# The load stage of a gated Hedgehog attention kernel: query and key weights first, blocks of w_phi from the host, x stores behind the x loads

## The chip, the cores and the metric

One core of a Trainium2 chip. The metric is the device time of one execution in microseconds (us), the median of several runs. TensorE is called PE, its weight loads PEld, VectorE DVE, ScalarE ACT, GpSimd POOL, and the engine that issues most transfers SP. Each engine runs its own list of instructions strictly in the order in which it was written out when the program was built; semaphores hold an instruction until what it needs is there.

## What is computed

With x of 2048 rows and 576 columns, all in float32:

```
xn  = layernorm(x)
q, k, v = heads of xn @ wqkv                      # 32 heads of 18
pq, pk  = q @ w_phi[h], k @ w_phi[h]              # w_phi: 32 x 18 x 18
phi_q, phi_k = [softmax(p), softmax(-p)] each
s   = ((phi_q (phi_k^T v)) / (phi_q (phi_k^T 1) + 1e-6)) @ wo
B   = (silu(xn @ w_gate) * (xn @ w_up)) @ w_down  # 4608 hidden columns
out = x + s * silu(B)
```

pq and pk are linear in xn, so the kernel folds w_phi into the query and key weights before it multiplies them with x ("fold").

## The kernel before, in words

Products that must be as exact as float32 are made of float32r parts: each operand is split into a high part (a cast on ACT) and a low part (a subtraction on DVE or POOL), and the products high-high, high-low and low-high are summed in PSUM. `split_rows` does this for a weight that lies in two full chunks of 128 rows and a tail of 32; the tail's correction is a third, narrow DVE instruction.

The 2048 rows of x are four blocks of 512 rows: blocks 0 and 1 form the first half (i = 0), blocks 2 and 3 the second (i = 1). A normalised and transposed block lies in two "places" of `xpool`, X10 and X11 for block 2, X12 and X13 for block 3, X00 to X03 for blocks 0 and 1; a place holds 128 partitions of 5 x 512 numbers (two high chunks, the tail, two low chunks).

The load stage, which is all that the change touches, does the following.

- `load_x(b)` loads a block as four tiles `xn` of 128 rows. `norm_stats` makes mean and variance on DVE (two BN_STATS and a BN_AGGR per tile), the square root on ACT and five small DVE steps behind it; for blocks 0 and 1 together one such chain serves eight tiles. `norm_block` scales the tiles (two on DVE, two on ACT), repeats the tail columns on POOL, transposes the block on PE (24 transposes into three PSUM tiles `tp`), and splits the result into the X places (ACT cast, DVE subtraction; the tails by DVE for block 3 and by POOL for the others). ACT stores an unsplit copy of the tails, `x_dram`.
- `load_fold(m)` loads key (m = 0) or query (m = 1) weights in five groups of 126 rows (the last has 72), `fold` multiplies each group on PE with the block-diagonal matrix PHI of seven heads (six matmuls a group into a `tp` tile, which the profile counts as twelve) and splits it into KVWH/KVWL or QH/QL. Before, POOL makes PHI from w_phi (`phi_s`) and a mask of ones.
- `early_weights` and `early_tile` use blocks 2 and 3 at once: for the first two chunks of 128 hidden columns they multiply gate and up with x (PSUM tiles `pe`, 14 matmuls of 512 columns for gate and 14 for up; a "half tile" here is both for one block). They depend on one x block and on two loads `raw`.
- `keep_clock(n)` issues n matmuls of zeros whose result nobody reads.
- `keep_x` stores three X places of the second half to `a_dram`; they are read back some 800 us later.

At the end of the stage PE starts the key products (`k_tile`, tile `p2`; "p L94" in the profile), which need the folded key weights and block 2, and from which on the change leaves the order on every engine as it is.

The order on the engines is set by a scheduler when the program is built: it works through the program with its own estimates of durations; `tc.high_priority()` lets an instruction go ahead, `tc.issue_after(x)` holds one behind x, and what is written is otherwise its preference. The chip does not reorder the lists. PSUM tiles `tp` exist three times, `xn` eight times, `wst` (weights as loaded) five times before; a new use waits until the readers of the old one are done. At most eight transfers of SP and ACT together are under way: each takes the next of eight semaphores (DMAHW0 to DMAHW7) and waits until that one's last transfer has landed.

## Time and profile before

| what | value |
|---|---|
| median of 3 runs | 1603.73 us (1602.67 to 1605.22) |
| profiled execution, its own time / span | 1603.6 us / 1601.7 us |
| PE busy in the span | 1590.1 us (99%) |
| DVE, ACT, POOL busy | 73%, 45%, 41% |
| idle matmuls (L148) | 31 from 1.00 us, 6 from 14.78 us |
| first transpose of block 2 / of block 3 | 11.40 / 29.56 us |
| fold of the key weights from / of the query weights from | 16.21 / 53.78 us |
| first key product on PE | 66.59 us |

The profile is one execution. A timeline row has its start, how long the merged pieces took, engine, line, operation, written tile <- read tiles, shapes, count, and in brackets the idle time before it with what ended it. A row of groups has count, busy time and mean duration in ns. A row of a stretch has its length and each engine's busy time with the instruction count. Matmul durations overlap, so a count of starts over a time tells the pace. An idle engine costs nothing unless the others wait for it.

### The profile page before, as it was taken

Reading aid. Unit: us, or ns where it says so; the run is one execution under the profiler, and the core shown is the slowest. Engines: PE = TensorE matmul, PEld = TensorE weight load, DVE = VectorE, ACT = ScalarE, POOL = GpSimd, SP = SyncE. Lnnn points to the kernel's source line nnn. Section 1 sums busy time; section 2 is a strip of 40 time slices with the busy share of each in tenths; the row PEclk is TensorE's granted clock in tenths of the full one; section 3 lists DMA queues with packets and bytes.
Section 4 is the critical chain, followed back from the end, with each engine's and each line's share of the span. In section 5 each row is a group of like instructions: output and inputs, shape, how many; then the busy total and the mean of one; then the engine's idle time right before and its main releaser. Section 6 shows DMA issues by size and latency. Waiting matters only on the chain.

```text
span 1601.7 us, 25319 instructions
## 1 busy us (share of the span) xinstructions
PE 1590.1 (99%) x9415; PEld 1420.7 (89%) x9415; DVE 1176.5 (73%) x1729; ACT 724.9 (45%) x1404; POOL 663.7 (41%) x714
## 2 busy tenths in 40 slices
PE   9999999999999999999999999999999999999998
PEld 6899998999988888888888888888888888888887
DVE  7777769889866778987777778635667656666577
ACT  5633345444435654544444444455343333333334
POOL 3676662434115535544535445223324324133133
PEclk9999999999999999999999999999999999999999
DMA  9522243436438454455545453874545565556435
GB/s 313 189 81 80 91 145 115 126 108 189 127 132 280 164 192 165 164 180 189 179 163 201 171 180 124 325 229 139 163 138 146 183 193 158 171 181 187 143 117 178
DMA packets 123181, 268.29 MB, mean 168 GB/s; under 512 B 12978, under 2 KB 54066, under 8 KB 121778
## 3 DMA queue, kind: packets, MB, share of 16 engines
q1 hardware_dynamic: 107612, 244.73, 46.5%
q0 software_dynamic: 3552, 12.59, 2.7%
q10 hardware_dynamic: 11894, 9.35, 1.8%
q8 instruction: 74, 1.21, 0.3%
q14 instruction: 49, 0.40, 0.1%
HBM read 167.53 MB, written 99.09 MB: 166 GB/s over the span
## 4 chain that ended last, share of the span: by engine, by line
PE 92%; DVE 3%; POOL 2%; DMA 2%; ACT 1%; issue 1%; SPq 0%; ACTq 0%; DVEq 0%; POOLq 0%
PE pd L875 25%; PE px L758 24%; PE pw L758 12%; PE py L758 6%; PE p L94 6%; PE pe L94 5%; PE p L651 4%; PE kvp L330 2%; PE po L631 2%; PE vx L418 1%; PE pt L625 1%; POOL slo L363 1%; PE vy L94 1%; PE vx L94 1%; DMA wst<-in_A_w_qk 0%
## 5 line engine op out<-in xcount | busy, mean ns | idle before, releaser
L875 PEld LDWEIGHTS pd<-dw,hh 128*128 128x128 f32 x3012 | 424.0, 188 | 22.2 <-ACT pd L922 1.5
L875 PE MATMUL pd<-dw,hh 128*128 128x288 f32 x3012 | 438.5, 295 | 1.4 <-ACT pd L922 0.7
L758 PE MATMUL px<-X,w 128*128 128x512 f32 x1512 | 386.5, 390 | 0.0
L758 PEld LDWEIGHTS px<-X,w 128*128 128x128 f32 x1512 | 274.6, 188 | 49.1 <-ACT s L787 2.3
L758 PE MATMUL pw<-X,w 128*128 128x512 f32 x744 | 190.7, 392 | 0.0
L758 PEld LDWEIGHTS pw<-X,w 128*128 128x128 f32 x744 | 138.6, 188 | 29.4
L792 DVE TENSOR_TENSOR s<-pw,s 128x512 f32<-128x512 f32 x126 | 86.4, 687 | 97.7 <-ACT s L787 86.4
L1029 DVE TENSOR_TENSOR acc<-pd,acc 128x576 f32<-128x576 f32 x128 | 96.2, 753 | 76.9 <-PE pd L875 76.4
L787 ACT COPY s<-px 128x512 f32<-128x512 f32 x126 | 73.6, 584 | 156.7 <-PE px L758 156.7
L61 DVE TENSOR_TENSOR hh<-ha,hh 128x512 fp32r<-128x512 f32 x140 | 111.3, 821 | 21.8 <-ACT hh L60 21.4
L60 ACT CAST hh<-ha 128x512 fp32r<-128x512 f32 x140 | 82.7, 619 | 87.6 <-PE pd L875 74.3
L1001 POOL TENSOR_TENSOR hb<-hb 128x512 f32<-128x512 f32 x34 | 46.5, 1367 | 160.6 <-DVE hb L804 159.6
L94 PE MATMUL pe<-X,wh 128*128 128x512 f32 x340 | 107.0, 395 | 0.3 <-ACT wh L64 0.3
L61 DVE TENSOR_TENSOR w<-ld,w 128x512 fp32r<-128x512 f32 (+1 forms) x96 | 80.5, 839 | 34.2 <-ACT w L60 32.9
L758 PE MATMUL px<-X,wt 128*128 128x512 f32 x252 | 98.1, 389 | 0.0
L758 PE MATMUL py<-X,w 128*128 128x512 f32 x378 | 97.0, 391 | 0.0
L988 POOL TENSOR_TENSOR h<-ha,hb 128x512 f32<-128x512 f32 x34 | 44.6, 1313 | 124.2 <-DVE ha L808 94.1
L1014 POOL TENSOR_TENSOR ha<-ha 128x512 f32<-128x512 f32 x34 | 52.6, 1563 | 97.2 <-DVE hh L61 97.2
L60 ACT CAST w<-ld 128x512 fp32r<-128x512 f32 (+1 forms) x96 | 52.8, 550 | 87.3 <-POOL ld L746 57.2
L812 ACT COPY py<-px 128x512 f32<-128x512 f32 x63 | 36.0, 572 | 103.8 <-PE px L758 74.9
L743 POOL TENSOR_TENSOR ts<-ld 128x256 f32<-128x256 f32 x32 | 27.6, 864 | 127.0 <-issue 71.4
L758 PEld LDWEIGHTS py<-X,w 128*128 128x128 f32 x378 | 67.8, 188 | 10.7
(286 smaller groups left out, 3256.1 us busy)
## 6 DMA issues: line engine op xcount, KB each, us to landing
w_dram<-w SPq DMA_DIRECT2D x90, 512.0 KB
w<-w_dram SPq DMA_DIRECT2D x90, 512.0 KB
wt<-t_dram SPq DMA_DIRECT2D x62, 336.0 KB
ld<-in_B_w_gu SPq DMA_DIRECT2D x32, 512.0 KB
rt<-in_B_w_down SPq DMA_DIRECT2D x33, 288.0 KB
rb<-in_B_w_down SPq DMA_DIRECT2D x33, 288.0 KB
w_dram<-w SPq DMA_DIRECT2D x30, 256.0 KB
w<-w_dram SPq DMA_DIRECT2D x30, 256.0 KB
```

The source lines that it names most:

```text
L60: nc.scalar.copy(hi, src)
L61: nc.vector.tensor_sub(lo, src, hi)
L94: last = nc.tensor.matmul(ps, l, r, start=n == 0, stop=n == len(pairs) - 1)
L651: nc.tensor.matmul(ps[:, 0:HALF], a[0:w, g, jc], bw[0:w, g, n], start=k == 0, stop=k == 3 * NG - 1)
L758: nc.tensor.matmul(ps, l, r, start=first and n == 0, stop=last and n == len(mm) - 1, skip_group_check=True)
L787: snaps.append(nc.scalar.copy(t, ps))
L792: nc.vector.tensor_add(t, ps, t)
L875: nc.tensor.matmul(ps, l, r, start=first and n == 0 and m == 0, stop=n == len(hs) - 1 and m == 2, skip_group_check=True)
L988: sub(s, g["h"][0][0], g["h"][0][1])
L1001: nc.gpsimd.tensor_add(a21, a21, g["h"][1][1])
L1014: sub(a12, a12, g["h"][0][0])
L1029: nc.vector.tensor_add(a2, pd[:, :, 0:HALF], a2)
```

## The change

The host lays w_phi out as five blocks of 126 x 126 with the heads on the diagonal, so that PHI is one load and POOL's products are gone. The key weights are the first loads on SP, then block 2, the query weights, the first gate and up weights, block 3. Weights come into the X0 places, three groups to a place, which are free until blocks 0 and 1 are transposed. The key fold stands before everything else; two groups of the query fold stand before block 2's transposes, three behind them. Of the idle matmuls 8 are left. The value weights have six buffers instead of five. The three `a_dram` stores are held behind the last x load. Line numbers of the load stage move by up to four; L216 (transposes) becomes L212, L249 (folds) L248, L186 (statistics) L182.

```diff
-    XB = [[xpool.tile([P, 5, BT], F32R, name=f"X{i}{j}") for j in range(4)] for i in range(2)]
+    XB = [None, [xpool.tile([P, 5, BT], F32R, name=f"X1{j}") for j in range(4)]]
...
-                phi_s = prep.tile([GW, NG, DH], F32, name="phi_s")
-                PHI = prep.tile([GW, NG, GH, DH], F32, name="PHI")
-                wf = w_phi.rearrange("h d f -> (h d) f")
+                PHI = prep.tile([GW, NG, GW], F32, name="PHI")
...
-                        nc.sync.dma_start(xn[:, 0:D], xf[i * P:(i + 1) * P, :])
+                        loads.append(nc.sync.dma_start(xn[:, 0:D], xf[i * P:(i + 1) * P, :]))
...
                     for g, (o, w) in enumerate(GROUPS):
-                        ws.append(prep.tile([GW, 6 * P], F32, name="wst", bufs=5))
-                        nc.sync.dma_start(ws[g][0:w], w_qk[m, o:o + w])
+                        if g % 3 == 0:
+                            rows = xpool.tile([P, 5, BT], F32, name=f"X0{2 * m + g // 3}").rearrange("p c n -> p (c n)")
+                        ws.append(rows[0:w, g % 3 * 6 * P:(g % 3 + 1) * 6 * P])
+                        nc.sync.dma_start(ws[g], w_qk[m, o:o + w])
...
-                keep_clock(31)
+                keep_clock(8)
+                nc.scalar.dma_start(PHI, w_phi)
+                nc.scalar.dma_start(ident, ident_in)
+                wk = load_fold(0)
                 xns = load_x(2)
-                nc.scalar.dma_start(phi_s[:, 0:4, :], wf[0:4 * GW, :].rearrange("(g p) f -> p g f", p=GW))
-                nc.scalar.dma_start(phi_s[0:D - 4 * GW, 4, :], wf[4 * GW:D, :])
-                for g, (o, w) in enumerate(GROUPS):
-                    nc.gpsimd.tensor_mul(PHI[0:w, g], phi_s[0:w, g, :].unsqueeze(1).to_broadcast([w, GH, DH]), mask[0:w])
-                wk = load_fold(0)
+                wq = load_fold(1)
+                nc.scalar.dma_start(mask, mask_in)
+                fold(wk, KVWH, KVWL, range(NG))
+                norm_stats([2], xns[0:4])
+                fold(wq, QH, QL, range(2))
+                _, rest, copy = norm_block(2, xns[0:4])
+                folded = fold(wq, QH, QL, range(2, NG))
+                first_weights = [early_weights(0, rest, copy)]
                 xns += load_x(3)
-                norm_stats([2], xns[0:4])
-                last, rest, _ = norm_block(2, xns[0:4])
-                with tc.issue_after(last.ins):
-                    keep_clock(6)
                 with tc.issue_after(rest.ins):
                     norm_stats([3], xns[4:8])
-                first_weights = [early_weights(0)]
-                fold(wk, KVWH[:, :, :, 0:D], KVWL[:, :, :, 0:D])
                 _, _, copy = norm_block(3, xns[4:8])
...
-                wq = load_fold(1)
-                fold(wq, QH, QL)
                 norm_block(1, xns[4:8])
-                for f in range(2):
-                    early_tile(f, 1, first_weights[f], store=nc.gpsimd, hold=None if f else norms[3])
+                with tc.issue_after(folded.ins):
+                    for f in range(2):
+                        early_tile(f, 1, first_weights[f], store=nc.gpsimd, hold=None if f else norms[3])
...
             def keep_x():
-                for n, j in enumerate((0, 1, 3)):
-                    nc.sync.dma_start(a_dram[n], XB[1][j].bitcast(F32))
+                with tc.issue_after(loads[-1].ins):
+                    for n, j in enumerate((0, 1, 3)):
+                        nc.sync.dma_start(a_dram[n], XB[1][j].bitcast(F32))
...
+    phi = np.zeros((NG, GH, DH, GH, DH), np.float32)
+    for h in range(H):
+        phi[h // GH, h % GH, :, h % GH] = np.asarray(inputs["A_w_phi"])[h]
...
+            "A_w_phi": phi.reshape(NG, GW, GW).transpose(1, 0, 2),
```

How this moves instructions, at three places. First PE, at the start of its list, behind the first idle matmuls. Before (`tp<-ident,xn` are transposes, `tp<-PHI,wst` a fold, `pe<-X_64` half tiles; X_64 is X10):

```order
L148 MATMUL pe<-idle 128x512
L216 MATMUL tp<-ident,xn 128x128 x24
L148 LDWEIGHTS idle
...
L249 MATMUL tp<-PHI,wst 128x126 x18
L94 MATMUL pe<-X_64,wh 128x512 x2
```

Now (X_118 and X_122 are key weights in X00 and X01, X_133 and X_137 query weights in X02 and X03, X_60 is X10):

```order
L147 MATMUL pe<-idle 128x512
L248 MATMUL tp<-PHI,X_118 128x126 x18
L248 MATMUL tp<-PHI,X_122 128x126 x6
L248 MATMUL tp<-PHI,X_122 128x72 x6
L248 MATMUL tp<-PHI,X_133 128x126 x12
L212 MATMUL tp<-ident,xn 128x128 x24
L248 MATMUL tp<-PHI,X_133 128x126 x6
L248 MATMUL tp<-PHI,X_137 128x126 x6
L248 MATMUL tp<-PHI,X_137 128x72 x6
L94 MATMUL pe<-X_60,wh 128x512
```

The transposes of block 2, which came first, stand behind the whole key fold and two groups of the query fold.

Second, DVE at the normalisation of block 2, from the last tile's statistics to the scaling. Before:

```order
L186 BN_STATS stats<-xn 128x6
L187 BN_AGGR mv<-stats 128x2 [waits DVE_49]
L190 TENSOR_SCALAR mv<-mv 128x4 [waits DVE_49]
L192 RECIPROCAL rs<-rs 128x4 [waits Activation_49]
L193 TENSOR_TENSOR rt<-rs 128x4 [waits DVE_49]
```

Now (QL and QH are the split of the first two query groups):

```order
L182 BN_STATS stats<-xn 128x6
L65 TENSOR_TENSOR QL<-tp,QH 128x4x126 [waits Activation_49]
L183 BN_AGGR mv<-stats 128x2 [waits DVE_49]
L66 TENSOR_TENSOR QH<-tp,QH 32x2x126
L186 TENSOR_SCALAR mv<-mv 128x4 [waits DVE_49]
L65 TENSOR_TENSOR QL<-tp,QH 128x4x126 [waits Activation_49]
L188 RECIPROCAL rs<-rs 128x4 [waits Activation_49]
L66 TENSOR_TENSOR QH<-tp,QH 32x2x126
L189 TENSOR_TENSOR rt<-rs 128x4 [waits DVE_49]
```

The two query groups now stand inside the chain that ends in the scale of block 2. On ACT, both QH casts and a table load stand before the square root in the same way.

Third, DVE at the normalisation of block 3, now. Between the steps of its root stand the statistics of block 0's first tiles, each with a wait for its load:

```order
L182 BN_STATS stats<-xn 128x6 [waits DMAHW1_49]
L186 TENSOR_SCALAR mv<-mv 128x4 [waits DVE_49]
L182 BN_STATS stats<-xn 128x6
L188 RECIPROCAL rs<-rs 128x4 [waits Activation_49]
L183 BN_AGGR mv<-stats 128x2 [waits DVE_49]
L182 BN_STATS stats<-xn 128x6 [waits DMAHW2_49]
L189 TENSOR_TENSOR rt<-rs 128x4 [waits DVE_49]
...
L182 BN_STATS stats<-xn 128x6 [waits DMAHW3_49]
...
L200 TENSOR_SCALAR xn<-xn,mv,rs 128x576 x2
```

Before, the root of block 3 was mixed with the splits of the key weights (KVWL, KVWH) instead, and the statistics of block 0 came behind the scaling.

18 lines of the change are left out of this document (9 added, 9 removed).

## The prediction

> **What bounds the kernel now.** I read the page first, then two stretches of the span (busy time of PE, PEld, DVE, ACT, POOL; granted clock, DMA share, GB/s), then the chain of waits, PE's timeline, and last DMA, DVE and ACT in the first part alone.
>
> ```profile
> 0.00:66.60 66.60, 62.82 (x366) 48.47 (x366) 51.78 (x118) 43.20 (x60) 25.30 (x53) 1.00 0.88 290
> 66.60:330.00 263.40, 262.94 (x1904) 250.67 (x1905) 207.60 (x290) 111.88 (x234) 151.25 (x182) 1.00 0.33 104
> ```
>
> From 66.6 us on PE idles 0.5 us in 263 us, and from there on the change leaves every engine its instructions in the same order. A shift of the first key product therefore moves the end by as much; nothing behind it takes a delay back. Only the first 66.6 us decide. The chain of waits, then PE's timeline, then the half tiles between 37 and 46 us:
>
> ```profile
> 5.28 7.74 DMA wst<-in_A_w_qk
> 66.59 3.99 PE p L94 x28
> ...
> 1.00 9.70 PE L148 MATMUL pe<-idle 128*128 128x512 bf16 x31 [1.00 <-POOL idle L143]
> 11.40 0.44 PE L216 MATMUL tp<-ident,xn 128*128 128x128 f32 x2 [0.70 <-DVE xn L204]
> 14.78 1.46 PE L148 MATMUL pe<-idle 128*128 128x512 bf16 x6
> 16.21 4.28 PE L249 MATMUL tp<-PHI,wst 126*128 126x126 f32 x36
> 29.56 2.81 PE L216 MATMUL tp<-ident,xn 128*128 128x128 f32 x24
> 53.78 5.52 PE L249 MATMUL tp<-PHI,wst 126*128 126x126 f32 x48
> 37.00:46.00 9.00, 9.00 (x41) 7.45 (x40) 0.69 (x1) 1.19 (x2) 1.00 1.02 372
> ```
>
> Useful PE work starts at 11.40 with the transposes of the first x block (block 2). It is four blocks of transposes (2.8 us each, 11.2 us), two folds of five groups (5.52/4 = 1.4 us a group, 7.0 us a fold) and four half tiles of gate and up (28 matmuls each; 9.00/41 = 0.22, by the starts 0.2275 us, so 6.4 us each, 25.5 us). That makes 50.7 us of the 55.2 us from 11.40 to 66.59. To be had are the first 11.4 us, the 1.5 us of idle matmuls and 3 us of gaps. DVE is nearly as full: it is busy 51.8 of 66.6 us, and between 15 and 50 us almost without a break. These are its groups in that window (count, busy us, mean ns):
>
> ```profile
> L186 DVE BATCH_NORM_STATS2 stats<-xn 128x6 f32<-128x288 f32 x24 | 9.3, 428 | 0.0
> L204 DVE TENSOR_SCALAR xn<-xn,mv,rs 128x576 f32<-128x576 f32 x5 | 2.9, 594 | 0.0
> L65 DVE TENSOR_TENSOR KVWL<-tp,KVWH 128x504 fp32r<-128x504 f32 x4 | 2.7, 670 | 0.1
> L187 DVE BATCH_NORM_AGGREGATE mv<-stats 128x2 f32<-128x12 f32 x12 | 2.4, 198 | 0.1
> L66 DVE TENSOR_TENSOR KVWH<-tp,KVWH 32x252 fp32r<-32x252 f32 x4 | 1.7, 418 | 0.1
> L228 DVE TENSOR_TENSOR X<-tp,X 32x512 fp32r<-32x512 f32 x2 | 1.3, 678 | 0.0
> ```
>
> **The change, part by part.** *Removed:* 29 of 37 idle matmuls, and POOL's five products for PHI (2 us, off the chain). That by itself gains nothing; it only lets the folds start when their operands land. *The x stores* (three of 1280 KB, 3.93 MB, 10.6 us at the 372 GB/s of the last PE row) go behind the x loads. I cost that at nothing, since DVE waited for x loads 4.7 us in all, 3.9 of them before the first tile:
>
> ```profile
> DVE stats L186 <- DMA xn<-in_A_x: 4.7, 3, 3.9
> ```
>
> Without that cover, it is the upper bound of a gain, 0.8 us; behind the loads the stores run while PE works, and their reader is in the second half.
>
> *When the work can start.* PE's order is now: fold K (five groups), two groups of fold Q, and only then the transposes of block 2. These can no longer come before the second query load has landed. DMA rates by stretch, and the landing of the last tile of block 2 in the kernel before:
>
> ```profile
> 0.00:2.00 2.00, 1.00 0.11 22
> 3.00:4.00 1.00, 1.00 1.08 372
> 0.00:6.30 6.30, 1.00 0.72 216
> 8.00:13.00 5.00, 1.00 1.00 257
> 7.96 0.82 DVE L186 BATCH_NORM_STATS2 stats<-xn 128x6 f32<-128x288 f32 x2 [0.24 <-DMA xn<-in_A_x]
> ```
>
> Data flow from 2.0 us. Tiles of x move at 372 GB/s; while the key weights (126 rows) are loaded, at 8 to 13 us, the rate is 257 with the engines fully busy. By 6.3 us 1.36 MB had moved, which is block 2 and the three small tables; its last tile was awaited until 7.96. So data count as landed 1.7 us after their turn. In the changed kernel there lie ahead, in the order of issue: PHI 0.32 MB, key weights 1.77, block 2 with the tables 1.31, two query groups 0.77. The 2.86 MB of weights take 11.1 us at 257, the 1.31 MB 3.5 us at 372: 2.0 + 11.1 + 3.5 + 1.7 = 18.3 us. If weights moved at 372 like x it would be 14.9; that is the low end.
>
> [...]
>
> *From the landing to the first transposes.* Fold group 1.4 us (19.7). ACT then casts QH, loads the table for the square root, and takes the root; before, that load was over at 4 us. These rows price it:
>
> ```profile
> 2.76 1.28 ACT L191 ACT_TABLE_LOAD   x1 [2.76 <-issue]
> 9.53 0.20 ACT L191 ACTIVATE rs<-mv 128x4 f32<-128x4 f32 x1 [5.48 <-DVE mv L190]
> 14.93 2.36 DVE L219 TENSOR_TENSOR X<-tp,X 128x1024 fp32r<-128x1024 f32 x2 [3.10 <-ACT X L218]
> 55.38 0.82 ACT L64 CAST QH<-tp 128x756 fp32r<-128x756 f32 x1
> ```
>
> 0.8 + 1.3 → 21.8. From the root to the first transpose it was 11.40 − 9.53 = 1.9 us, plus 0.4 for the row correction that now stands between: 24.1 us, against 11.40. Ahead of it is then 7.0 + 2.8 us of folding that before came later, so PE has 12.7 us less of lead and 9.8 us less to do (and 1.5 of idle matmuls): about 1.4 us lost before any new gap.
>
> *New gaps.* PE's next group of fold Q needs a PSUM buffer that DVE frees 16.21 − 11.40 = 4.8 us after the first transpose (in the kernel before, six idle matmuls filled that): 28.9; three groups, 33.1; a half tile, 39.5. Then PE's next instruction is the transposes of block 3, and DVE is not ready for them. DVE has X10 and X11 split 17.3 − 11.4 = 5.9 us after the first transpose, at 30.0. In its new order there follow, before the first scaled tile of block 3: statistics of block 3 (8 × 0.39 + 4 × 0.2 = 3.9), two raw splits (2 × 1.09, priced as the KVWL and KVWH rows, = 2.2), three groups of QL (2.9), the statistics of three tiles of block 0 that stand between the steps of the root (2.9), six small steps (1.0), the scaling (0.6): 13.5 us, so 43.5. PE waits 4 us. All of this waits for no load: by the same count the third tile of block 0 lands at about 38 (3.86 MB of weights at 257, 7.2 MB of the rest at 372, 2.0 and 1.7).
>
> Behind it PE has 8.4 us of transposes and three half tiles, 27.5 us in all. The tails of X12 and X13 (the 678 ns rows) stand on DVE behind the statistics of the first tile of block 1, whose load is issued only when block 3's transposes release the buffer and takes some 3 us from issue to use (0.74 to 3.95 at the start); PE has 11 matmuls to fill, and waits 2.2 us. DVE's remaining 9 us to the scaling of block 0 leave PE another 0.8 us. Together 30.5: the first key product at 74.0 us, 7.4 us later than 66.59.
>
> **The sum.** The profiled execution took 1603.6 us (span 1601.7), the median of the runs is 1603.73, so no correction: 1603.6 + 7.4 = **1611.0 us**.
>
> **Rivals.**
> *The early start pays.* PHI and the first key group (0.70 MB) land at 2.0 + 2.8 + 1.7 = 6.5 us; if PE then were as dense as before (50.7 us and 3 us of gaps) the key products would begin at 60.2, 6.4 us earlier: 1597.2. For it: the stage is mostly PE work, and DMA was saturated. Against it: the fixed order on PE, ACT and DVE that ties block 2 to the query loads. 10%.
> *A wash.* Weights move at 372, block 2's transposes start at 20.7, and DVE keeps up, so that block 3 follows the half tile at 20.7 + 15.4 = 36.1: the key products begin at 66.6, and the time is 1603.6. For it: DVE's list could run tighter than its means. Against it: the 257 row. 17%.
> *PE slows in its gaps.* PE stands idle some 4 us before block 2's transposes and 4 us before block 3's, with no idle matmuls. In the row of the 31 idle matmuls the first ten took 4.45 us and the other 21 only 5.25:
>
> ```profile
> 1.00 4.45 PE L148 MATMUL pe<-idle 128*128 128x512 bf16 x10 [1.00 <-POOL idle L143]
> ```
>
> So PE starts slow, at about twice the time of one, though the granted clock reads 1.00 throughout. If each gap puts it back there, two sets of transposes (2.8 us each) take twice as long on the path: 1616.6. Against it: the gaps may be too short or broken. 13%.
> [...]
>
> **How the numbers follow.** The forecast has 60%; its own range is 1607 (loads at 372, 3.4 us less) to 1614. The range 1605 to 1617 takes in the slow clock and the upper half of the wash, and leaves out the early start. A difference counts from 0.2% (3.2 us), about what this kernel's measurement can tell. Faster: the early start, 0.10. Same: the wash and a little of the forecast's low end, 0.19. Slower: 0.71.
>
> **What would show it.** In the changed profile: the first transpose of block 2 near 24 us, with PE idle before it and ACT loading a table; PE idle again before block 3's transposes with DVE named as releaser; the first key product near 74; the rest unchanged. If the key weights move at well above 257 GB/s, or the transposes of block 2 start before 19 us, the sum is wrong in its first term; if PE shows no gap before block 3, in its second.

## The result, and the profile after

| | before | changed |
|---|---|---|
| median of 4 runs each, same chip | 1603.76 us (1602.67 to 1605.22) | 1619.95 us (1617.89 to 1620.55) |
| ratio, 95% interval | | 1.0098 (1.0086 to 1.0111) |
| profiled execution / its span | 1603.6 / 1601.7 us | 1620.55 / 1618.7 us |
| first transpose of block 2 | 11.40 us | 26.04 us |
| first transpose of block 3 | 29.56 us | 46.93 us |
| first transpose of block 0 | 47.45 us | 68.91 us |
| first key product | 66.59 us | 83.60 us |

The change made the kernel 16 us slower; 1611.0 had been forecast (range 1605 to 1617). First the two stretches of the span in the profile after, columns as in the prediction (busy us of PE, PEld, DVE, ACT, POOL with counts; granted clock, DMA share, GB/s):

```profile
0.00:83.60 83.60, 64.46 (x337) 53.06 (x337) 54.56 (x117) 45.06 (x61) 24.06 (x49) 0.88 0.71 234
83.60:347.00 263.40, 262.77 (x1904) 250.52 (x1903) 206.00 (x290) 111.84 (x234) 150.77 (x182) 1.00 0.33 104
```

Behind the first key product PE idles 0.6 us in 263 again, with the same 1904 instructions. So the whole loss is the 17.0 us by which that product comes later (83.60 − 66.59; 1620.55 − 1603.6 = 16.95). But the clock in the first stretch reads 0.88, where before it read 1.00. PE's timeline up to the first key product, with the gaps in brackets:

```profile
1.00 3.57 PE L147 MATMUL pe<-idle 128*128 128x512 bf16 x8 [1.00 <-POOL idle L142]
...
17.10 4.55 PE L248 MATMUL tp<-PHI,X 126*128 126x126 f32 x24 [3.16 <-DMA X<-in_A_w_qk]
26.04 5.55 PE L212 MATMUL tp<-ident,xn 128*128 128x128 f32 x24 [4.38 <-issue]
31.81 4.24 PE L248 MATMUL tp<-PHI,X 126*128 126x126 f32 x36 [0.23 <-DVE X L215]
...
46.93 5.45 PE L212 MATMUL tp<-ident,xn 128*128 128x128 f32 x24 [4.46 <-DVE xn L200]
...
56.63 0.73 PE L94 MATMUL pe<-X,wh 128*128 128x512 f32 x2 [1.50 <-DVE X L224]
...
68.91 1.02 PE L212 MATMUL tp<-ident,xn 128*128 128x128 f32 x3 [1.35 <-DVE xn L200]
...
83.60 0.29 PE L94 MATMUL p<-KVWH,X 128*128 128x288 f32 x1
```

The gaps stand where they were forecast. What was not in the forecast are the durations: 24 transposes take 5.5 us where block 3's 24 took 2.81 before, and two query groups of 12 matmuls each take 4.55 where the forecast had 2.8. The granted clock, in stretches cut at these places (the last three columns are clock, DMA share, GB/s):

```profile
14.00:17.00 3.00, 0.00 (x0) 0.00 (x0) 2.93 (x10) 0.50 (x1) 0.00 (x0) 1.00 1.02 268
18.00:21.00 3.00, 3.00 (x17) 3.00 (x16) 1.25 (x4) 0.79 (x1) 0.00 (x0) 0.51 1.03 255
26.00:31.00 5.00, 4.96 (x23) 4.67 (x24) 0.89 (x2) 2.56 (x4) 2.22 (x8) 0.50 0.99 369
46.00:52.00 6.00, 5.07 (x23) 4.81 (x24) 3.59 (x10) 5.11 (x6) 2.85 (x9) 0.50 0.00 0
69.50:72.50 3.00, 3.00 (x10) 2.41 (x10) 1.64 (x3) 2.76 (x4) 2.64 (x7) 0.50 0.19 27
```

Behind four of its gaps (3.16, 4.38, 4.46 and, at 68.91 us, 1.35 us) PE runs at half its clock for some 3 to 6 us; behind the gap of 1.50 us at 56.63 it does not (1.00 from 53 to 69 us). The rate of the loads is as forecast (255 and 268 GB/s while weights are loaded, 369 behind them). The second loss that the forecast had not priced stands on DVE. Its rows behind block 3, and POOL's in the same time:

```profile
55.90 1.28 DVE L224 TENSOR_TENSOR X<-tp,X 32x512 fp32r<-32x512 f32 x2
57.21 1.92 DVE L65 TENSOR_TENSOR wl<-raw,wh 128x512 fp32r<-128x512 f32 x1
59.16 1.55 DVE L66 TENSOR_TENSOR wh<-raw,wh 32x256 fp32r<-32x256 f32 x1
...
63.85 0.68 DVE L65 TENSOR_TENSOR wl<-raw,wh 128x512 fp32r<-128x512 f32 x1
64.56 1.98 DVE L66 TENSOR_TENSOR wh<-raw,wh 32x256 fp32r<-32x256 f32 x1
```

```profile
57.16 3.27 POOL L281 TENSOR_TENSOR KVWL<-wst,KVWH 128x576 fp32r<-128x576 f32 x2 [5.56 <-ACT KVWH L278]
60.75 1.44 POOL L281 TENSOR_TENSOR KVWL<-wst,KVWH 128x576 fp32r<-128x576 f32 x1 [0.32 <-ACT KVWH L278]
64.24 0.56 POOL L134 DMA_DIRECT2D h_dram<-h  x1 [2.06 <-DVE h L133]
64.82 1.44 POOL L281 TENSOR_TENSOR KVWL<-wst,KVWH 128x576 fp32r<-128x576 f32 x1
```

The subtraction that takes 0.68 at 63.85 takes 1.92 while POOL subtracts; its narrow sister takes 1.55 and 1.98 instead of 0.42. That is 3.9 us (1.92 + 1.55 + 1.98 − 0.69 − 0.42 − 0.42) on a DVE that has to scale block 0 before PE can go on.

### The profile page after: what moved, and what is told of

The parts are those of the page before. It is cut to its first block, busy times and chain, and to the rows that moved or that the text cites. A ratio compares the mean times of both kernels' runs of the same rounds, so it can differ in the third digit from the quotient of the medians.

```text
span 1618.7 us, 25243 instructions
## 1 busy us (share of the span) xinstructions
PE 1591.6 (98%) x9386; PEld 1425.7 (88%) x9386; DVE 1175.9 (73%) x1729; ACT 726.8 (45%) x1405; POOL 664.3 (41%) x709
## 3 DMA queue, kind: packets, MB, share of 16 engines
q8 instruction: 74, 1.21, 0.3%
## 4 chain that ended last, share of the span: by engine, by line
PE 92%; POOL 1%; DVE 1%; issue 0%; ACT 0%; DMA 0%; DVEq 0%; ACTq 0%; POOLq 0%
PE px L758 25%; PE pd L875 24%; PE pw L758 12%; PE py L758 6%; PE p L94 6%; PE pe L94 5%; PE p L651 4%; PE kvp L329 2%; PE po L631 2%; PE vx L418 1%; PE pt L625 1%; POOL slo L363 1%; PE vy L94 1%; PE vx L94 1%; PE vw L418 0%
```

## The experiments

The theories at the start: *order* (the forecast's: block 2 is tied to the query loads, DVE comes late to block 3), *clock* (PE at half speed behind its gaps), *port* (DVE slowed beside POOL; the word is a name only, no run shows what the two engines share). All comparisons are ratios to the kernel before on the same chip, five rounds each. Times of the four events in each profile, from PE's timelines, with the ratio:

| kernel | block 2 | block 3 | block 0 | key product | ratio (95%) |
|---|---|---|---|---|---|
| before | 11.40 | 29.56 | 47.45 | 66.59 | 1 |
| changed | 26.04 | 46.93 | 68.91 | 83.60 | 1.0098 (1.0086, 1.0111) |
| changed, idle matmuls in the gaps | 25.77 | 46.65 | 65.54 | 79.39 | 1.0080 (1.0066, 1.0094) |
| changed, no POOL subtractions | 26.69 | 47.75 | 66.23 | 79.75 | 1.0079 (1.0066, 1.0092) |
| both of these | 24.19 | 44.83 | 63.41 | 76.91 | 1.0070 (1.0057, 1.0083) |
| changed, table early | 23.73 | 43.73 | 64.78 | 78.30 | 1.0078 (1.0065, 1.0091) |
| changed, statistics late | 25.23 | 44.67 | 63.96 | 77.50 | 1.0081 (1.0068, 1.0094) |
| idle matmuls, table, statistics | 23.10 | 41.24 | 60.42 | 73.46 | 1.0048 (1.0035, 1.0061) |
| changed, query fold behind block 2 | 22.78 | 45.97 | 64.94 | 77.70 | 1.0073 (1.0060, 1.0087) |
| changed, raw weights behind block 3's x | 25.43 | 45.74 | 67.20 | 81.83 | 1.0100 (1.0087, 1.0113) |
| changed, block 2 first | 12.13 | 45.05 | 63.70 | 77.22 | 1.0070 (1.0057, 1.0083) |
| … and query fold late | 11.69 | 34.77 | 55.81 | 75.24 | 1.0072 (1.0059, 1.0084) |
| … and query loads late | 12.02 | 35.05 | 56.24 | 77.75 | 1.0061 (1.0049, 1.0074) |
| … and block 3's x ahead of raw weights | 11.49 | 30.32 | 49.25 | 68.16 | 1.0027 (1.0016, 1.0037) |
| key weights first, query as before | 20.98 | 38.00 | 58.84 | 80.34 | 1.0094 (1.0078, 1.0109) |
| before, few idle matmuls | 10.88 | 31.22 | 50.45 | 69.22 | 1.0027 (1.0016, 1.0037) |

Events of kernels with the same front part differ by up to 1.5 us from execution to execution (block 2 at 25.23 to 26.69 in the three that leave it alone), so a row's single event is not read closer than that. Each ratio is known to about ±0.13%, so the difference of two changed kernels is known to about ±0.18% (2.9 us): a single cure that gains 0.2% stands at the edge of that, and where a cause is named below, it is the durations in the traces that carry it. The profiled execution of the changed kernel is also some 1 us above what its ratio gives (1.0098 × 1603.6 = 1619.3 against 1620.55), so gains read from its profile are that much too large; verdicts go by the ratios.

**Clock: idle matmuls in the gaps.**

```diff
-                fold(wk, KVWH, KVWL, range(NG))
+                lastk = fold(wk, KVWH, KVWL, range(NG))
+                with tc.issue_after(lastk.ins):
+                    keep_clock(10)
...
-                fold(wq, QH, QL, range(2))
+                lastq = fold(wq, QH, QL, range(2))
+                with tc.issue_after(lastq.ins):
+                    keep_clock(12)
...
                         ps = pps.tile([P, 2, BT], F32, name="tp", bufs=3)
+                        if b == 3 and c == 0:
+                            with tc.issue_after(roots[-1].ins):
+                                for _ in range(8):
+                                    nc.tensor.matmul(ps[:, 0], idle, idle.unsqueeze(1).to_broadcast([P, BT // P, P]), start=True, stop=True)
```

> The changed kernel with idle matmuls put back in PE's three gaps: 10 behind the key fold, 12 behind the first two query groups, 8 ahead of block 3's transposes. They go to PSUM buffers that are free there; on every other engine the order of instructions is the same, so nothing else changes. Clock theory: what the changed kernel loses beyond its order comes from PE's granted clock, which reads 0.50 in the trace for 3.5 us at 18 us, 5.8 us at 25.5 and 6.2 us at 46, each behind a gap of 3.2 to 4.5 us. With the gaps filled the clock stays at 1.00, the first two query groups take 2.9 us instead of 4.55, block 2's and block 3's transposes 2.8 instead of 5.5: 1.5 + 1.0 (the rest of block 2's is hidden behind DVE's splits) + 2.6 = 5 us, so 1614 to 1616 against 1620. Order theory: PE waits for loads and for DVE in any case, the slow clock costs nothing that the wait would not; within 1 us of the changed kernel, 1619 to 1621.

Measured 1615.27, 1.0080. PE's rows:

```profile
14.67 2.32 PE L147 MATMUL pe<-idle 128*128 128x512 bf16 x10
17.92 1.57 PE L252 MATMUL tp<-PHI,X 126*128 126x126 f32 x12 [0.93 <-DMA X<-in_A_w_qk]
19.82 1.57 PE L252 MATMUL tp<-PHI,X 126*128 126x126 f32 x12 [0.33 <-DMA X<-in_A_w_qk]
21.23 2.75 PE L147 MATMUL pe<-idle 128*128 128x512 bf16 x12
...
26.36 4.27 PE L216 MATMUL tp<-ident,xn 128*128 128x128 f32 x22 [0.18 <-POOL xn L203]
...
47.29 2.91 PE L216 MATMUL tp<-ident,xn 128*128 128x128 f32 x22 [0.20 <-POOL xn L203]
```

Where the clock held, the work took its old time: query groups 1.57 each, block 3's transposes 2.91 for 22. Block 2's fell again (4.27), behind a rest of 1.8 us of gap. The first key product came 4.2 us earlier, nearly all of it behind block 3: from its transposes to the key product 32.7 us instead of 36.7. In front, nothing was won, because in this execution the second query group landed only at 19.8. The expected 5 us was 4.2 in the profile and 3 in the ratio. Not all of that is the clock's: in this kernel DVE comes to the first raw split behind block 3 before POOL's subtractions start (0.69 and 0.42 us at 55.14 and 55.86, where the changed kernel has 1.92 and 1.55), and the two raw splits are 2.4 us too long together instead of 3.9. So the clock is a part of the loss, and its size is not cleanly shown.

**Clock, in the order of the kernel before.**

```diff
-                keep_clock(31)
+                keep_clock(8)
...
-                with tc.issue_after(last.ins):
-                    keep_clock(6)
```

> The kernel before with the idle matmuls cut as in the change: 8 at the start instead of 31, and none instead of 6 behind block 2's transposes; loads, folds and the order of the x blocks as in the kernel before (some neighbours on DVE and ACT change places behind 16 us). Clock theory: PE stands idle from 4.6 us to 11.4, so block 2's transposes and what follows run at a granted clock of 0.50 for 5 to 7 us, and the end comes 2 to 3.5 us later: 1606 to 1607. Order theory: the idle matmuls hide nothing, 1603 to 1605.

Measured 1606.69, 1.0027, as the clock theory had it. PE's row and the granted clock in that stretch:

```profile
10.88 5.47 PE L216 MATMUL tp<-ident,xn 128*128 128x128 f32 x24 [6.28 <-DVE xn L204]
```

```profile
11.00:16.00 5.00, 5.00 (x23) 4.73 (x24) 1.70 (x3) 3.02 (x4) 2.11 (x8) 1.00 1.05 297
```

The transposes take twice their time, though this stretch's granted clock reads 1.00: after the kernel's start the records seem to miss a slow phase that the durations show (the first ten idle matmuls, quoted in the prediction, are of the same sort). So the idle matmuls of the kernel before were worth 4 us there; the forecast had costed their removal at nothing.

**Port: no POOL subtractions.**

```diff
-                for (k, c), src in zip(places[0:4], wv):
-                    with tc.issue_after(rests[-1].ins):
-                        nc.gpsimd.tensor_sub(KVWL[:, k, c, D:2 * D], src, KVWH[:, k, c, D:2 * D])
...
+                nc.gpsimd.memset(KVWL[:, :, :, D:2 * D].bitcast(F32), 0.0)
```

> The changed kernel without POOL's four subtractions that make the low parts of the value weights (their place is set to zero at the start instead, so the values lose their low parts); every other engine keeps its instructions and their order. Port theory: DVE's subtractions of the raw gate and up weights take 1.92, 1.55 and 1.98 us beside them instead of 0.69, 0.42 and 0.42, 3.9 us in all on a DVE that is full from 55 to 68 us; without them the scaling of block 0 comes 2.5 to 3.9 us earlier (64.3 to 65.7 instead of 68.19) and the end 2 to 4 us: 1.0073 to 1.0086 of the kernel before, where the changed kernel is 1.0098. Rival: DVE waits elsewhere for what it wins, since block 1's tiles land when they do; less than 1 us, 1.0092 to 1.0100.

Measured 1616.74, 1.0079. DVE's same instructions:

```profile
57.84 0.69 DVE L65 TENSOR_TENSOR wl<-raw,wh 128x512 fp32r<-128x512 f32 x1
58.56 0.42 DVE L66 TENSOR_TENSOR wh<-raw,wh 32x256 fp32r<-32x256 f32 x1
...
62.12 0.68 DVE L65 TENSOR_TENSOR wl<-raw,wh 128x512 fp32r<-128x512 f32 x1
62.84 0.42 DVE L66 TENSOR_TENSOR wh<-raw,wh 32x256 fp32r<-32x256 f32 x1
```

All back to their own durations, block 0 scaled at 65.50 instead of 68.19, and from block 3 to the key product 32.0 us instead of 36.7. A control stands in the same trace: the raw split before block 3, which runs beside POOL's correction of the tails, was not touched by the edit and is as long as in the changed kernel (1.21 and 1.39 us at 35.02 and 36.26). So what the port theory expected came, as far as durations go: 1.92, 1.55 and 1.98 us beside POOL's subtractions, 0.69, 0.42 and 0.42 without them. With DVE on time the slow spell at 69 us is gone too (granted clock 1.00 from 66 to 72), so the 4.7 us are not DVE's alone: from block 3's to block 0's first transpose it is 18.5 us instead of 22.0, and from there to the key product 13.5 instead of 14.7.

**Both together.** The edit is the sum of the two.

> The changed kernel with idle matmuls in its three gaps and without POOL's four subtractions for the low parts of the value weights (their place is zero, so the values lose their low parts). Alone the first moved the first key product from 83.60 to 79.39, the second to 79.75. If slow clock and DVE beside POOL are two separate losses, together they bring it to 75 to 76.5 (the stretch from block 3's transposes to the first key product from 36.7 us to 28 to 30, where the forecast had 30.5), 1.0045 to 1.006. If the slow spell at 69 us is only a consequence of the late DVE, both save the same: 78 to 79.5, above 1.007.

Measured 1613.78, 1.0070: on the border between the two cases. The key product came at 76.91, but 1.9 us of that is block 2, which came earlier in this execution. From block 3 to the key product it is 32.1 us, hardly less than with one cure (32.7 and 32.0). PE's row says why:

```profile
45.47 4.54 PE L216 MATMUL tp<-ident,xn 128*128 128x128 f32 x22 [0.20 <-POOL xn L203]
```

The idle matmuls did not hold the clock this time: 22 transposes took 4.54 us, where they had taken 2.91. Without these 1.6 us it would be 30.5, the forecast's figure; but that is worked out, not run. That the two losses add up is not shown: by the ratios both cures together gain 4.5 us (1.0098 to 1.0070), each alone about 3.

**Order in front: the query fold behind block 2, the table early, the statistics late.** Three edits of the changed kernel:

```diff
-                fold(wq, QH, QL, range(2))
-                _, rest, copy = norm_block(2, xns[0:4])
-                folded = fold(wq, QH, QL, range(2, NG))
+                last, rest, copy = norm_block(2, xns[0:4])
+                with tc.issue_after(last.ins):
+                    folded = fold(wq, QH, QL, range(NG))
```

> The changed kernel with all of the query fold behind block 2's transposes (the loads in their old places): block 2 waits for the key loads and its own x tiles, not for the second query group. Order theory: x of block 2 lands at about 14.5 us, the first transpose comes at 19 to 21 instead of 26.04; three quarters of the 6 us pass to the end, 1614 to 1616; but the query fold's 7 us of PE and its splits on DVE then stand between block 2 and block 3, so 1617 is still order theory. Clock theory alone: PE still has a gap of 4 to 6 us before block 2 and another one before block 3, so the clock falls there as before; less than 2 us gained, 1618 to 1620.

```diff
+                nc.vector.memset(rt, 1.0)
+                nc.scalar.activation(rs[:, 0:1], rt[:, 0:1], AF.Sqrt)
                 keep_clock(8)
```

> The changed kernel with a square root of a constant on ACT at the very start, so that its table is loaded before data come and not between the query casts and block 2's root. Chain theory: the root comes 1.3 us earlier (and ahead of the second query cast, 0.8 more): first transpose of block 2 at 23.9 to 24.8 instead of 26.04, and because DVE's chain follows from it without slack, the end 1.2 to 2.1 us earlier: 1.0085 to 1.0090. Rival: it is eaten by the PSUM and DVE waits behind it, below 0.5 us.

```diff
-                norm_stats([0, 1], xns)
+                with tc.issue_after(scales[3].ins):
+                    norm_stats([0, 1], xns)
```

> The changed kernel with the statistics of blocks 0 and 1 held until block 3 is scaled, so that the three tiles of block 0 (2.9 us of DVE) no longer stand between the steps of block 3's root. DVE theory: block 3's transposes start 2.9 us earlier (44.0 instead of 46.93), and PE's gap there falls from 4.46 us to 1.6, so its clock does not fall either (2.6 us less of transposes); but the same work then stands between 47 and 55 us, where DVE had 3.7 us without work, so most of it is hidden: 3 to 5.5 us gained, 1.0064 to 1.0079 of the kernel before. Conservation: DVE is the bound from 47 to 69 us as well, and the statistics only move: 0 to 1.5 us, 1.0089 to 1.0098.

Measured 1614.84 (1.0073), 1616.32 (1.0078) and 1617.13 (1.0081). The order theory is borne out in each: block 2 at 22.78 in the first (later than the 19 to 21 expected), at 23.73 in the second, block 3 at 44.67 in the third (44.0 expected). By the ratios the gains at the end are 3.2 us for the table, where block 2 came 2.3 us earlier (1.3 expected, or 2.1 with the cast), and 4.0 us for the fold, where it came 3.3 earlier; that the end gains more than the front is within the noise. In all three profiles block 0's transposes run at full clock (2.77 us for 21 in the last two), where the changed kernel was at half around 70 us. A few us lost in front may so set off a slow spell behind; by the traces it costs 1.2 us (14.7 us from block 0's first transpose to the key product in the changed kernel, 13.5 in the kernels with the table early, with the statistics late and without the subtractions, which all run it at full clock).

**Three cures at once.**

> The changed kernel with three cures at once: the square root's table loaded at the start, the statistics of blocks 0 and 1 behind block 3's scaling, and idle matmuls in the gaps (10, 8 and 8). Alone they moved the first key product from 83.60 to 78.30, 77.50 and 79.39. If they are different losses they add up: 68 to 70 us, about 1.002. If they are the same loss seen from three sides (each only brings block 3 or the clock out of the slow spell at 69 us): 74 to 77, 1.005 to 1.0065. The forecast's own model of the change, which knew no slow clock, had 74.0.

Measured 1611.09, 1.0048, between the two cases and nearer to "the same loss". It is the one kernel with the new order in which the clock reads 1.00 in the whole stage:

```profile
0.00:30.00 30.00, 23.20 (x153) 17.02 (x154) 16.20 (x41) 12.97 (x19) 3.16 (x14) 1.00 0.92 286
30.00:73.00 43.00, 39.18 (x211) 30.62 (x210) 37.21 (x79) 29.98 (x44) 19.93 (x35) 1.00 0.74 256
```

Its key product comes at 73.46. That it lies where the forecast lay (74.0) vindicates no term: two of its three cures take away what the forecast had counted (table 1.3, statistics 2.9). The raw splits behind block 3 hardly meet POOL in it either (0.69, 0.41, 0.68 and 0.82 us). So with the clock at 1.00 and DVE nearly undisturbed there the kernel still loses 0.48%: by this trace what is left is mostly the order's.

**Which part of the order costs: taken back step by step.** First block 2 in front, with the 31 and 6 idle matmuls:

```diff
-                keep_clock(8)
+                keep_clock(31)
...
-                wk = load_fold(0)
                 xns = load_x(2)
+                wk = load_fold(0)
...
-                fold(wk, KVWH, KVWL, range(NG))
                 norm_stats([2], xns[0:4])
-                fold(wq, QH, QL, range(2))
-                _, rest, copy = norm_block(2, xns[0:4])
-                folded = fold(wq, QH, QL, range(2, NG))
+                last, rest, copy = norm_block(2, xns[0:4])
+                with tc.issue_after(last.ins):
+                    keep_clock(6)
+                fold(wk, KVWH, KVWL, range(NG))
+                folded = fold(wq, QH, QL, range(NG))
```

> The changed kernel with block 2 loaded and transposed first, as in the kernel before, and its 31 and 6 idle matmuls; the rest of the change stays: PHI from the host in blocks, weight rows in X places, both folds ahead of block 3, stores later. Order theory: the loss is the wait of block 2 for 2.9 MB of weights; first transpose back at 11.4, first key product at 66 to 71: 1.000 to 1.003 of the kernel before. Rival: the early query fold itself costs (DVE gets all ten groups' splits, 11 us, before block 3), so block 3 still comes 5 us or more late and the time stays above 1.005.

Measured 1615.76, 1.0070: the order theory as I had put it falls, the rival's result came. Block 2 is back at 12.13, 14 us earlier, and block 3 comes only 2 us earlier, at 45.05. Besides the 7 us of the query fold, a part of what stands between is seen on PE and ACT:

```profile
22.52 2.87 PE L248 MATMUL tp<-PHI,X 126*128 126x126 f32 x24 [0.29 <-issue]
29.44 0.98 PE L248 MATMUL tp<-PHI,X 126*128 126x126 f32 x3 [4.05 <-ACT KVWH L64]
```

```profile
25.44 0.83 ACT L64 CAST wh<-raw 128x768 fp32r<-128x768 f32 x1 [2.38 <-DMA raw<-in_B_w_gu]
26.57 0.83 ACT L64 CAST wh<-raw 128x768 fp32r<-128x768 f32 x1 [0.29 <-DMA raw<-in_B_w_gu]
27.31 1.20 ACT L64 CAST KVWH<-tp 128x756 fp32r<-128x756 f32 x2
```

PE waits 4 us for casts of the key fold, which stand on ACT behind casts of raw gate and up weights; those wait for a load that SP issues behind the query weights. Then the fold of the query weights alone (with it goes the hold that kept the half tiles of blocks 0 and 1 behind it), and in a second kernel its loads too, go back to the place they had before:

```diff
-                folded = fold(wq, QH, QL, range(NG))
...
+                fold(wq, QH, QL, range(NG))
                 norm_block(1, xns[4:8])
```

> As the kernel with block 2 first: both loads of weights ahead of block 3's x tiles as there, but the query fold itself between the transposes of blocks 0 and 1. It parts the query weights' 1.77 MB (6.9 us at 257 GB/s) from their fold (7 us of PE, 5.3 us of DVE splits). If the loads are what makes block 3 late: its transposes stay near 45, the time near 1.007. Filler theory: x of block 3 lands at about 27, its transposes start at 33 to 36 and the first key product at 68 to 72: 1.001 to 1.004.

```diff
-                wq = load_fold(1)
-                folded = fold(wq, QH, QL, range(NG))
...
+                wq = []
+                for g, (o, w) in enumerate(GROUPS):
+                    wq.append(prep.tile([P, 6 * P], F32, name="wst", bufs=5)[0:w])
+                    nc.sync.dma_start(wq[g], w_qk[1, o:o + w])
+                fold(wq, QH, QL, range(NG))
                 norm_block(1, xns[4:8])
```

> As the kernel with block 2 first, but the query weights are loaded behind the value weights and folded between the transposes of blocks 0 and 1, as in the kernel before. Of the change there stay PHI from the host in blocks, the key weights in X places and the late stores. Filler theory (the query fold is PE's work while DVE normalises blocks 0 and 1; ahead of block 3 it is only delay): block 3's transposes back at 29 to 31, first key product at 66 to 68, 0.999 to 1.002 of the kernel before. Rival: something else that stays (PHI's 0.32 MB in front, the rows' places, the stores) costs, above 1.003.

Measured 1615.63 (1.0072) and 1612.80 (1.0061). Block 3 moved by 10 us, as the filler theory said for the first (34.77), but the key product only by 2: the 7 us of fold now stand behind block 0. The second contradicts the filler theory, which wanted 1.002 at most. Then block 3's x ahead of the raw weights:

```diff
                 wk = load_fold(0)
+                xns += load_x(3)
...
-                fold(wk, KVWH, KVWL, range(NG))
-                first_weights = [early_weights(0, rest, copy)]
-                xns += load_x(3)
...
                     norm_stats([3], xns[4:8])
+                first_weights = [early_weights(0)]
+                fold(wk, KVWH, KVWL, range(NG))
```

> As the kernel with block 2 first and the query fold between blocks 0 and 1, and now also the x tiles of block 3 ahead of the first raw gate and up weights, as in the kernel before. Of the change there stay PHI from the host in blocks, the key weights in X places and the late stores. If the order of work is all that costs: 0.999 to 1.002. If one of the three that stay costs: like the kernel without this last step, 1.0061.

Measured 1606.92, 1.0027: this step brings the key product from 77.75 to 68.16. It changes three things at once: the order of the loads, the hold of the raw casts behind block 2's row copy, and the place of the key fold, which now stands behind both. The first two alone, taken back in the changed kernel itself, give nothing:

```diff
+                xns += load_x(3)
...
-                first_weights = [early_weights(0, rest, copy)]
-                xns += load_x(3)
...
                     norm_stats([3], xns[4:8])
+                first_weights = [early_weights(0)]
```

> The changed kernel with this one step taken back: x of block 3 loaded ahead of the first raw gate and up weights (two transfers of 393 KB), whose casts no longer wait for block 2's row copy. If the raw weights standing in front are a loss of their own: block 3's transposes 2 to 4 us earlier (43 to 45 instead of 46.93), 1.007 to 1.0085. If not (x of block 3 has landed in time in the changed kernel, and DVE has the same work before block 3's scaling): 1.009 to 1.010.

Measured 1619.10, 1.0100, as the case without a loss had it. And the key weights ahead of block 2, with the query weights loaded and folded as before (the raw weights still in front of block 3's x), cost as much as the whole change:

```diff
-                keep_clock(31)
+                keep_clock(8)
...
+                wk = load_fold(0)
                 xns = load_x(2)
-                wk = load_fold(0)
...
+                fold(wk, KVWH, KVWL, range(NG))
                 norm_stats([2], xns[0:4])
```

(against the kernel with the late query loads; the fold's old place and the six idle matmuls are gone.)

> Half of the change: the key weights loaded and folded ahead of block 2 as in the change (8 idle matmuls), the query weights loaded late and folded between blocks 0 and 1 as in the kernel before. Filler theory: block 2's transposes at 17 to 20, but the key fold's 7 us of PE and 5.3 us of DVE are then done; block 3's at 31 to 35, first key product at 66 to 71: 1.000 to 1.003. Start theory (what counts is how late block 2 comes): 6 to 8 us late, 1.004 to 1.006.

Measured 1618.14, 1.0094: both expectations missed. So the parts do not add. The raw weights ahead of block 3's x, with the hold of their casts and the key fold in front, make block 3 5 us late (35.05 against 30.32); with the query weights in front as well it is 45.05, with the key weights instead 38.00, with all three 46.93, and from there taking the raw weights away gives 1.2 us and nothing at the end. Block 3 waits for the last of several things, and the removal of one uncovers the next. How the loss divides among these was not settled; the key weights or the query weights in front without the raw weights were not run on their own.

**What is left without the order: stores and PHI alone, on the kernel before.**

```diff
+                with tc.issue_after(loads[-1].ins):
                     for n, j in enumerate((0, 1, 3)):
                         nc.sync.dma_start(a_dram[n], XB[1][j].bitcast(F32))
```

> The kernel before with only the three stores of x moved behind the last x load. The prediction costs this at nothing, with 0.8 us of gain at most: 1602.9 to 1604.0. The rival: the stores now run while the first key products want their loads, and cost: above 1606.

```diff
-                nc.scalar.dma_start(phi_s[:, 0:4, :], wf[0:4 * GW, :].rearrange("(g p) f -> p g f", p=GW))
...
-                    nc.gpsimd.tensor_mul(PHI[0:w, g], phi_s[0:w, g, :].unsqueeze(1).to_broadcast([w, GH, DH]), mask[0:w])
+                nc.scalar.dma_start(PHI, w_phi)
```

> The kernel before with PHI made by the host and loaded as blocks (0.32 MB instead of 41 KB, ahead of block 2's tiles on the other queue), and POOL's five products gone; PE, DVE and SP keep their instructions and their order. What is left of the change when all orders are taken back cost 0.27%, 1.6 us at the first key product, and the late stores alone 0.3 us of that. If the rest is PHI's transfer in front of block 2: its last tile lands some 0.6 us later, the first transpose at 11.8 to 12.2 instead of 11.40, the first key product at 67.3 to 68.2: 1.0008 to 1.002. If it is the rows' places: within 0.3 us of the kernel before, 0.9995 to 1.0005.

Measured 1604.24, 1.0009 (1.0001 to 1.0018), and 1604.09, 1.0007 (0.9998 to 1.0016); key products at 66.91 and 65.88. Neither gains or loses 0.2%, as the prediction costed them. In the profile PHI's larger load does not delay block 2 (11.19). The last 0.27% of the step-by-step series is then not PHI or the stores alone, but the two together (0.16% if they add up) reach the lower end of its interval (0.16 to 0.37%), so a third cause is not shown. In its trace the root of blocks 0 and 1 comes 1.8 us late on ACT, behind a cast that waits for a value weight's load:

```profile
44.87 0.67 ACT L277 CAST KVWH<-wst 128x576 fp32r<-128x576 f32 x1 [2.98 <-DMA wst<-in_A_w_v]
45.45 0.59 ACT L129 ACTIVATE h<-pe 128x512 f32<-128x512 f32 x1
46.06 1.28 ACT L187 ACT_TABLE_LOAD   x1
47.36 0.21 ACT L187 ACTIVATE rs<-mv 128x8 f32<-128x8 f32 x1
```

That is a reading of one trace, not tested. No kernel tried is faster than the one before.

## Why the prediction was right in direction and wrong in size

*The frame held.* Only the first stretch counted, and its shift passed to the end one to one (17.0 and 16.95 us). The change was slower, for which the prediction had 0.71. What failed is the price of the work in that stretch: the sum took PE at full clock behind its new gaps, put the removed idle matmuls at nothing, and took DVE's splits at durations without POOL beside them. The first key product came at 83.60 us instead of 74.0, and the largest miss is the last step, from block 3's transposes to that product, 36.7 us instead of 30.5.

*When the work can start.* Forecast 18.3 us for the landing of the second query group. In three executions with idle matmuls its landing can be read from PE, which folds the second group at about 18.2 without a wait, at 18.64 and at 19.82 behind one. The rate of 257 GB/s held (255 and 268 above).

*From the landing to the first transposes.* Forecast 24.1, measured 26.04. The path was right (ACT's casts, a table load of 1.28 us, the root; the early table moved block 2 to 23.73). The term that was too small is the fold in front, taken at 1.4 us a group; at half clock two groups took 4.55 us instead of 2.8, 1.7 us more. That a fast PE would have had block 2 earlier by as much is a reading of one trace: with idle matmuls the groups took 1.57 us each, and block 2 came at 25.77 all the same, behind a later landing.

*New gaps.* The gap before block 3 was forecast at 4 us with DVE as the releaser; it is 4.46, and DVE is named. From block 2 to block 3 I had 19.4, measured 20.9. Two things made it longer: two DVE rows beside POOL's correction of the tail (1.21 and 1.39 us at 34 us, instead of 0.69 and 0.42: 1.5 us), and block 2's transposes at half clock, behind which DVE had X10 and X11 split 6.8 us after the first transpose instead of 5.9 (0.9 us). The rest of DVE's list was 0.9 us shorter than my means.

*Behind block 3.* This step failed most: 30.5 forecast, 36.7 measured. Its transposes took 5.45 us instead of 2.8, and DVE's raw splits beside POOL 3.9 us more than alone; a part of both is hidden. Without POOL's subtractions the way from block 3 to block 0 is 3.5 us shorter, the slow spell behind block 0 costs 1.2, and 1.5 us remain for block 3's transposes at half clock, close to the 1.6 worked out from the kernel with both cures. The durations in my sum were means from a window of the kernel before, where PE ran at full clock and only one such split met POOL (1.64 us at 39.71, against 0.69 at 36.55); these means did not hold at a place where POOL stood beside them.

| | us beyond the forecast | shown by |
|---|---|---|
| to block 2: query groups at half clock | 1.9 | one trace; the run with idle matmuls gave nothing here |
| block 2 to block 3: DVE beside POOL 1.5, transposes at half clock 0.9, rest of DVE −0.9 | 1.5 | one trace |
| block 3 to block 0: DVE beside POOL | 3.5 | the kernel without the subtractions (18.5 us instead of 22.0) |
| block 0 to the key product: slow spell | 1.2 | 13.5 us instead of 14.7 in three kernels at full clock |
| block 3's transposes at half clock | 1.5 | what remains; with idle matmuls they took 2.91 us for 22 in one kernel |
| sum | 9.6 | 83.60 − 74.0 = 9.6 |

The sum agrees because its rows were split up to agree, and each event is uncertain by 1 us and more. By the ratios, the two cures together took away 4.5 (give or take 2.9) of the 8.3 us between the forecast (1.0046) and the result (1.0098), with the clock still at half behind two gaps. So some half of the miss is shown by runs; the rest is read from one trace.

*Removed idle matmuls* were costed at nothing. In the order of the kernel before they are worth 0.27%.

*Rivals.* "PE slows in its gaps" had 13% and 1616.6. Its mechanism came true, but it is only part of the miss: of block 2's transposes it wanted 2.8 us and 0.9 passed on, of block 3's 2.8 and some 1.5, and it knew neither the slow query groups nor the slow spell; DVE beside POOL stood in no rival. That 1616.6 lies near the time is in part luck. I had set it low because the gaps might be too short or broken. They were not: behind 4.38 and 4.46 us the clock read 0.50. That no row of the kernel before shows a second slow phase says nothing against it: that kernel has no gap of that length behind its start (0.70 us is its longest in the stage), since its idle matmuls fill it, and the clock column, which I had read as 1.00 throughout, reads so even in the start's slow phase (ten idle matmuls in 4.45 us, the other 21 in 5.25). "The early start pays" and "a wash" found no support: PE did fold at 6 us, but block 2's transposes came 14.6 us later for it, which was more than the 9.8 us of folding that were then done.

## What to carry to other kernels

In this case work moved into the idle start of the stage did not help, because the first useful block fell behind it. Before such a move ask what that block would then wait for in every engine's fixed list, ACT's casts and SP's loads among them. Before idle matmuls or other fillers are taken out, price the work behind each new gap at half the TensorE clock (behind gaps of 4.38 and 4.46 us 24 transposes took 5.55 and 5.45 us here, where they had taken 2.81), and set off against it only what the profile shows to be hidden. Before a DVE duration goes into a sum, see what POOL does at the new place: the raw splits, which read two SBUF tensors, took 0.69 us alone and up to 1.92 beside POOL's subtractions.

## What the runs showed of the hardware that was not expected

*Short gaps were enough for the clock here.* In the kernel with idle matmuls PE stood idle for only 1.8 us (24.0 to 25.8) and ran little up to 26.4; then the clock was at half:

```profile
26.50:29.50 3.00, 3.00 (x15) 3.00 (x16) 0.00 (x0) 0.62 (x2) 1.46 (x7) 0.50 1.01 381
```

In the changed kernel it fell at 69 us behind gaps of 0.6 and 1.35 us that followed each other closely. So it fell behind gaps of under 2 us, and did not fall behind one of 3: in the kernel with the statistics late, PE stood idle for 2.99 us before block 3's transposes, and the clock read 1.00 from 40 to 60 us. Whether a gap of some 1.4 us was followed by a slow clock differed between two executions (22 of block 3's transposes in 2.91 us in one kernel with idle matmuls, in 4.54 us in the other, with gaps of 1.37 and 1.46 us before them). What decides it was not found.

*DVE beside POOL.* In the changed kernel's load stage only the splits of the raw weights grow, from 0.69 to as much as 1.92 us and from 0.42 to 1.98; they read two SBUF tensors. The statistics, which read one, keep their time beside the same POOL instruction (three in 1.13 us at 60.86, and in 1.13 at 59.13 in the kernel without the subtractions), and so do the splits that read one operand from PSUM: in the kernel before, QL's take 0.68 us at 56.23 and 57.48 beside POOL's correction of the tails (55.66 to 58.15). That the number of SBUF operands decides was not tested.
